# One block's keys and queries cast to fp16 before they are turned, in an attention and gated-FFN kernel

## The chip, the cores and the metric

The kernel runs on one core of one Trainium2 chip. The core has five instruction streams that run side by side and wait for each other by semaphores: PE (TensorE, matrix products), ACT (ScalarE), DVE (VectorE), POOL (GpSimd) and SP (SyncE, which here only issues loads and stores). The metric is the device time of one execution in microseconds (us), the median over several runs.

## What is computed

Inputs are q, k and v of 4 batches, 8 heads, 768 positions and 64 values per head, in fp32, and three weight matrices of a gated feed-forward layer. Cut to what matters:

```python
k_min, k_max = k_chunks.min(3), k_chunks.max(3)          # chunks of 32 positions
ub = sum(maximum(q * k_min, q * k_max))                  # bound of each query for each chunk
top_chunks = argsort(where(causal, ub, -1e9))[..., -6:]  # six chunks for each query
scores = where(sel & (i >= j), (q @ k.T) / 8, -1e9)
x = softmax(scores) @ v                                  # 3072 tokens of 512 values
out = (sigmoid(x @ w_gate) * (x @ w_val)) @ w_out        # d_ff 1536
```

The first 128 positions of a batch see at most four chunks, so nothing is chosen for them: they are plain causal attention.

## The kernel before

**Stages.** The 24 blocks of 128 tokens are spread over eight units of three blocks, u0 to u7. A unit is prepared (keys and queries turned so that the head's 64 values lie on partitions, bounds `ub`, the choice of chunks, masks), attended (scores `sc_`, `exp_`, causal mask `cm_`, products with the values `pv_`, division `rz_` and `x_`), and sent through the feed-forward layer (`g_`, `tanh_`, `v_`, `hg_`, and the output products `o0_`, `o1_`, `o2_`). While PE does the feed-forward products of one unit, the next is attended and a later one prepared. `attend(units[2], ...)`, for instance, is interleaved with `ffn(units[1], ...)`.

**The first blocks of the batches.** The first block of each batch, positions 0 to 127, goes through its own function `first` (L593): four of them, b = 0 to 3; the one of b = 3 belongs to unit u2. `load_first` (L519) loads its k and q in two halves each (`kf0_3`, `kf1_3`, `qf0_3`, `qf1_3`) and v (`vf_3`), as fp32. `kfT_3` and `qfT_3` (L603) turn k and q on PE, by four products each with a 128x128 identity, into a PSUM bank; `kf16_3` (ACT) and `qf16_3` (DVE) copy these to fp16 (L607); `scf_3` makes the scores, `expf_3_*` and `cmf_3_*` the masked weights (L655, L658), `pvf_3_*` the products with the values (L665). `vc_3` (POOL) casts the values to fp16 (L631).

**Order.** Nothing is scheduled at run time. Each operation is entered with a list of engines that could do it, a cost for each, a priority and the buffers that it reads and writes (`plan.add`, L49). A planner has turned this into the long string `ORDER` (L94 to L273): a list of names, each with the buffers' numbers behind a colon and with `@ENGINE` where it isn't the first engine of its list. The names are issued in this order (`Plan.order`, L78), so each engine runs its own names in order, and a name whose inputs aren't ready holds up all later names of its engine. A buffer kind has a few numbered places (`ps`: 8 PSUM banks; `np`: 7 places for fp16 copies; `v`: 6 for landed blocks), and whoever is given a place waits until its last holder's users are done.

**POOL's queue around the block.** POOL does the causal masks (`cm_`, L879: a mask of the diagonal blocks of each head's weights, without which `pv_` of that head can't finish), casts of the values (`v16_`, L567), copies of keys and queries into the operands of the score products (`hk`, `hq`, `hqm`, all through the helper `copy`, whose lines are L345 for ACT, L347 for DVE, L349 for POOL), and loads of weights. Before the change its names run here in this order:

```
... k16_1_1 v16_0_5 hq1_u3_0 vc_3 hk1_1_3 hk0_1_3 cm_u2_7 v16_1_0 hq0_u3_0 hk1_1_1 cm_u2_0
cm_u2_6 hqm0_u3_2 hk1_1_0 cm_u2_4 hk1_1_2 hk0_1_2 hkp111 cmf_3_0 cmf_3_1 ...
```

Here `hq*_u3_*` and `hk*_1_*` are queries and keys of unit 3 and batch 1, `cm_u2_h` the mask of head h of unit 2. In unit 2 (blocks 4 and 5 of batch 0) a `pv_u2_h` is eleven products, 5 for the first block and 6 for the second; the last one of each block reads the masked diagonal.

**Pattern copies.** `hkp1eo` (L166) copies a constant pattern of 64 partitions x 1536 fp16 values from the operand of even batches to that of odd batches, four copies in all: `hkp110` and `hkp101` on DVE, `hkp100` and `hkp111` on POOL. Unit 3 is the first that reads them.

**PE's queue around the block**: `... ub_u3 pv_u2_1 sc_u2_4_1 kfT_3 sc_u2_4_0 g_u1_10 v_u1_10 sc_u2_6_0 g_u1_11 v_u1_11 sc_u2_6_1 o0_u1_0 o1_u1_0 qfT_3 sc_u2_6_2 sc_u2_4_2 pv_u2_0 sc_u3_1_1 sc_u3_1_0 o2_u1_0 o0_u1_1 pv_u2_7 pv_u2_4 ...`

Of the kernel before, what the change touches and what calls it, by code (L numbers as in the profile page):

```python
# [112 lines left out]
hq1_u1_1@POOL kx1_u2_3:1 ap1_u1 sc_u1_1_0:0,2 qm_u2_0@POOL:0 tanh_u0_1 v_u0_1:5 hg_u0_0 qm_u2_2@ACT kx1_u2_2
g_u0_2:4,2,2 hq1_u1_0@POOL kt_u2_2@DVE:1 hq0_u1_2@POOL kx1_u2_0 v_u0_2:3 tanh_u0_2 apt1_u1 hq0_u1_3@POOL exp_u1_1_0
g_u0_3:6,3,3 kx0_u2_2 v16_0_1 hg_u0_1 sc_u1_0_1:4,3 wo0 v_u0_3:2 hg_u0_2 tanh_u0_3 hk0_u2_3@ACT hkp110 sc_u1_0_0:0
hk1_u1_0@POOL exp_u1_0_1 g_u0_4:5,0,4 exp_u1_0_0 kx0_u2_0 sc_u1_3_2:6,1 kt_u2_0@DVE:2 sc_u1_2_2:3,0 sc_u1_3_1:4
exp_u1_3_2 sc_u1_2_0:0 qm_u2_1 exp_u1_3_1 kT_u2_1:7 qm_u2_3 v_u0_4:6 exp_u1_2_0 kx1_u2_1 kx0_u2_1 sc_u1_3_0:4 cm_u1_2
g_u0_5:0,1,5 hg_u0_3 exp_u1_3_0 hkp100@POOL v_u0_5:2 kt_u2_1:0 hq1_u2_3 tanh_u0_5 g_u0_6:4,2,6 tanh_u0_4 hq0_u2_1@POOL
hg_u0_5 sc_u1_0_2:7 v_u0_6:0 kcr_u2@POOL exp_u1_0_2 hg_u0_4 cm_u1_3 hqm1_u1_2@ACT sc_u1_1_2:5 cm_u1_0 g_u0_7:2,3,7
v16_0_3 v_u0_7:7 tanh_u0_7 wo2 tanh_u0_6 g_u0_8:6,1,8 hg_u0_7 hq0_u2_3 cm_u1_1 ub_u2:2,4 hq1_u1_3@DVE tanh_u0_8  # L120
hq0_u2_0@POOL exp_u1_2_2 hk1_u2_0@POOL sc_u1_2_1:7 v_u0_8:6 hqm1_u1_0 exp_u1_2_1 k11_1 exp_u1_1_2 g_u0_9:3,0,9
hq1_u2_1@POOL hg_u0_8 v_u0_9:7 tanh_u0_9 sc_u1_1_1:5 g_u0_10:6,3,10 hg_u0_9 ubn1_u2:0 v_u0_10:3 v16_0_2 tanh_u0_10
exp_u1_1_1 g_u0_11:7,1,11 v11 hg_u0_10 pv_u1_3:4 ubn0_u2 tanh_u0_11 pv_u1_2 mx1_u2:0 pv_u1_0:6 hk0_u2_1@ACT
sc_u1_5_2:5,1 v_u0_11:3 hk0_u2_2 exp_u1_5_2 hg_u0_6 hk1_u2_2@ACT wm_23 hg_u0_11 pv_u1_1 sc_u1_6_1:1,3 sc_u1_5_0:2
hq0_u2_2@DVE exp_u1_6_1 sc_u1_7_1:7,0 rz_u1_1:0 sc_u1_5_1:5 x_u1_1:1 exp_u1_7_1 sc_u1_6_0:0 rz_u1_0:0 exp_u1_6_0
sc_u1_4_1:3,2 hkp101 exp_u1_5_0 sc_u1_4_0:1 o0_u0_0:4,0 kcr1 mx0_u2 k10_1 exp_u1_5_1 xps_u1_1:7,1 cm_u1_5 o1_u0_0
hq1_u2_2 ap1_u2 exp_u1_4_1 ap0_u2 sc_u1_7_0:0 x_u1_0:0 sc_u1_6_2:2 o2_u0_0 exp_u1_7_0 apt1_u2:0 exp_u1_6_2
hqm1_u2_0@DVE exp_u1_4_0 xps_u1_0:5 o0_u0_1:3,1 osb_u0_0@DVE cm_u1_4 apt0_u2 out_u0_0 o1_u0_1 cm_u1_6 hqm0_u2_2@ACT
cm_u1_7 sc_u1_4_2:6 pv_u1_5:0 hqm0_u2_0 q01_1:1 exp_u1_4_2 pv_u1_6:2 sc_u1_7_2:1 hqm1_u2_2 kf0_3:5 pv_u1_4 exp_u1_7_2
sc_u2_1_0:4,1 rz_u1_2:0 sc_u2_3_2:6,3 xT_u1_0 sc_u2_3_0:1 exp_u2_1_0 x_u1_2:2 pv_u1_7 o2_u0_1 exp_u2_3_0 cm_u2_1  # L130
rz_u1_3:0 x_u1_3:1 exp_u2_3_2 xT_u1_1 sc_u2_1_1:5 k16_1_2:5 sc_u2_2_0:4,2 kx1_1_3:0 exp_u2_1_1 sc_u2_7_1:0,0
xps_u1_3:1 q10_1 xps_u1_2:2 k16_1_3:3 exp_u2_2_0 sc_u2_3_1:6 k16_1_0@DVE:2 q00_1 o0_u0_2:7,0 osb_u0_1 cm_u2_3 kt_1_3:0
hk0_u2_0@ACT cm_u2_2 o1_u0_2 exp_u2_7_1 xT_u1_3 xT_u1_2@ACT kx0_1_0 o2_u0_2 v_0_4:2 kx1_1_0 g_u1_0:5,0,12 v_u1_0:4
kt_1_0:6 tanh_u1_0 g_u1_1:3,3,13 kx0_1_1 sc_u2_2_1:0 v_0_5:4 v_u1_1:1 exp_u2_2_1 hg_u1_0 q11_1 g_u1_2:2,2,14 tanh_u1_1
kx0_1_2 hk1_u2_1@ACT v_u1_2:5 vf_3:1 exp_u2_3_1 kx0_1_3 osb_u0_2 g_u1_3:0,1,15 tanh_u1_2 sc_u2_7_0:4 tanh_u1_3
v_u1_3:3 hg_u1_2 kx1_1_2 sc_u2_1_2:6 v16_0_4 g_u1_4:7,0,16 vf1_3:4 kx1_1_1 sc_u2_2_2:2 k16_1_1:1 qf1_3:3 v_u1_4:0
tanh_u1_4 exp_u2_2_2 g_u1_5:5,2,17 v16_0_5 out_u0_2 hg_u1_4 kf1_3 v_u1_5:7 hg_u1_3 tanh_u1_5 out_u0_1 kt_1_2:2
exp_u2_1_2 g_u1_6:2,0,0 k11_2:0 sc_u2_7_2:0 hg_u1_5 v_1_0:0 v_u1_6:3 tanh_u1_6 qf0_u3_2:0 g_u1_7:5,1,1 hg_u1_6
pv_u2_2:6 qf0_u3_1 tanh_u1_7 pv_u2_3 qf0_u4_0:1 exp_u2_7_2 sc_u2_0_0:7,3 hk0_1_0@DVE v_u1_7:2 exp_u2_7_0 qf0_u3_3
exp_u2_0_0 g_u1_8:3,2,2 kcr_1 qf0_u3_0 qm_u3_2@ACT:0 sc_u2_0_1:5 hg_u1_1 v_u1_8:0 qf0_3 hq1_u3_0@POOL tanh_u1_8  # L140
qf0_u4_3 g_u1_9:4,0,3 qm_u3_0 k10_2 vc_3 kt_1_1:5 k01_2 v_u1_9:7 tanh_u1_9 hk1_1_3 sc_u2_0_2:1 hg_u1_7 ub_u3:3,4
exp_u2_0_2 hg_u1_8 hk0_1_3 exp_u2_0_1 cm_u2_7 pv_u2_1:2 ubn0_u3:0 sc_u2_4_1:1,2 v16_1_0 kfT_3:0 k00_2 qf0_u4_2
hq0_u3_0@POOL ubm0_u3 sc_u2_4_0:5 ubn1_u3 g_u1_10:3,3,5 kf16_3:3 mx0_u3:0 hk1_1_1 hq0_u3_2@ACT v_u1_10:4 hg_u1_9
cm_u2_0 sc_u2_6_0:0,1 exp_u2_4_0 ap0_u3 g_u1_11:7,1,4 v_1_1:2 tanh_u1_10 apt0_u3:0 v_u1_11:5 tanh_u1_11 ubm1_u3
hg_u1_10 hk0_1_1@ACT sc_u2_6_1:3 mx1_u3 o0_u1_0:7,0 hqm0_u3_0@ACT hg_u1_11 o1_u1_0 rz_u2_1:0 ap1_u3 exp_u2_6_0
qf0_u4_1 x_u2_1:0 qfT_3:4 exp_u2_6_1 q00_2:1 cm_u2_6 apt1_u3 sc_u2_6_2:5 hq1_u3_2@ACT hqm0_u3_2 sc_u2_4_2:0 pv_u2_0
hk1_1_0 rz_u2_0:0 exp_u2_6_2 sc_u3_1_1:6,3 qf16_3@DVE:1 exp_u2_4_2 sc_u3_1_0:3 o2_u1_0 x_u2_0:1 cm_u2_4 exp_u2_4_1
kx0_2_2 o0_u1_1:5,1 hk1_1_2 osb_u1_0 exp_u3_1_0 hqm1_u3_0@DVE hk0_1_2 out_u1_0 pv_u2_7:4 kx1_2_3:0 pv_u2_4:0 v_1_3:4
xps_u2_1:2,0 sc_u2_5_1:1,0 v_1_2:1 xT_u2_1@ACT hkp111@POOL hqm1_u3_2@DVE exp_u3_1_1 scf_3:7,3,2 o1_u1_1 q10_2
exp_u2_5_1 q11_2 pv_u2_6 expf_3_0 sc_u2_5_2:2 o2_u1_1 expf_3_1:1 cmf_3_0 rz_u2_3:0 x_u2_3:2 exp_u2_5_2 kx0_2_0 cmf_3_1  # L150
sc_u2_5_0:6 k16_2_0@ACT:0 pvf_3_0:1 sc_u3_0_0:7,2 v16_1_1 xps_u2_0:3 sc_u3_0_2:4 kx1_2_2 exp_u2_5_0 o0_u1_2:2,0
exp_u3_0_2 cm_u2_5 osb_u1_1 rzf_3_0:0 o1_u1_2 xT_u2_0 q01_2 cm_u3_1 kx0_2_3 exp_u3_0_0 v16_1_3 sc_u3_0_1:6 kt_2_0:5
v16_1_2 exp_u3_0_1 cm_u3_0 xf_3_0:0 pvf_3_1:4 sc_u3_1_2:3 pv_u2_5 sc_u3_2_1:5,0 xps_u2_3:7 o2_u1_2 exp_u3_2_1
k16_2_1:2 rz_u2_2:0 exp_u3_1_2 rzf_3_1:1 out_u1_1 x_u2_2:1 xT_u2_3@ACT xpsf_3_0:6 xf_3_1:2 pv_u3_1:1 xTf_3_0@ACT
sc_u3_3_0:5,1 kx1_2_0 sc_u3_3_1:3 xps_u2_2:0 pv_u3_0 xT_u2_2@ACT xpsf_3_1:7 sc_u3_5_0:4,2 rz_u3_0:0 xTf_3_1
k16_2_3@DVE:6 exp_u3_5_0 sc_u3_3_2:6 v_1_4:0 x_u3_0:0 exp_u3_3_1 sc_u3_6_0:0,3 g_u2_0:7,2,7 v_u2_0:4 hk1_2_0@ACT
kx1_2_1 g_u2_1:3,0,8 exp_u3_3_2 kt_2_1:1 exp_u3_3_0 tanh_u2_1 v_u2_1:1 kx0_2_1 k16_2_2@ACT:3 hg_u2_1 g_u2_2:6,3,9
tanh_u2_0 v_u2_2:5 kcr_2@POOL k11_3:0 osb_u1_2 cm_u3_5 qf1_u4_2 g_u2_3:3,1,10 qf1_u4_1 k01_3 exp_u3_6_0 qf1_u4_0
qf1_u4_3 qf0_u5_3:0 qm_u4_0@ACT:0 qm_u4_2@POOL kt_2_2:0 tanh_u2_2 v_u2_3:7 sc_u3_6_2:1 k00_3 exp_u3_6_2 hg_u2_0
g_u2_4:2,0,6 hq0_u4_0@ACT hq0_u4_2@POOL qf0_u5_0 tanh_u2_3 v_u2_4:0 xps_u3_0:6,1 ub_u4:1,4 qf0_u5_1 cm_u3_6  # L160
xT_u3_0@ACT hk0_2_2@DVE tanh_u2_4 hk0_2_1 k10_3 qf0_u5_2 g_u2_5:3,2,11 hg_u2_4 hq1_u4_2@POOL ubn0_u4:0 v_u2_5:6
ubm0_u4 cm_u3_3 ubn1_u4 v_1_5:5 hk1_2_2 hg_u2_3 g_u2_6:2,0,12 hg_u2_2 v_u2_6:0 hq1_u4_0@POOL pv_u3_3:1 kt_2_3:4
# [1091 lines left out]
```

## Time and profile before

| what | value |
|---|---|
| median of 3 runs | 285.15 us (285.08 to 285.25) |
| the profiled execution | 285.57 us |
| its span | 283.7 us, granted TensorE clock 1.0 |
| PE busy | 270.4 us, 95% |
| DVE, ACT, POOL busy | 234.3, 208.1, 115.4 us |
| HBM read, written | 30.67 and 6.29 MB |

All positions in time below are microseconds from the start of the span. A row of an engine's order of time gives the start, the duration, engine, line, operation, output<-inputs, shapes and how many; in square brackets stands how long the engine was idle before it and what ended that. The chain of waits is followed back from the last instruction, and its pieces give a start, a duration and what ran. Starts in it can lie some 0.1 to 0.2 us behind those of PE's own order of time, because PE's instructions overlap.

### The profile page before, as it was taken

The page shows a single profiled execution, that of the slowest core. Times are in us where ns is not written, and L with a number is a line of the kernel's source. Part 1 is how long each engine was busy: PE and PEld are TensorE (multiplying, and loading weights), DVE is VectorE, ACT ScalarE, POOL GpSimd, SP SyncE. Part 2 cuts the span into 40 slices and gives each one's busy share as a digit, 9 for nine tenths or more (in the row PEclk, how much of TensorE's full clock was granted, in tenths as well). Part 3 has the DMA queues.
Part 4 walks back from the last instruction along what each step waited for, and adds up shares of the span by engine and source line. Part 5 has one row for each costly group of instructions (what it writes and reads, how often), then busy time and mean ns, then how long its engine had stood idle before and what let it go on. Part 6 is the DMA issues. An engine that isn't in the chain of part 4 may idle for free.

```text
span 283.7 us, 7050 instructions
## 1 busy us (share of the span) xinstructions
PE 270.4 (95%) x2602; PEld 171.0 (60%) x2602; DVE 234.3 (83%) x643; ACT 208.1 (73%) x438; POOL 115.4 (41%) x184
## 2 busy tenths in 40 slices
...
GB/s 173 254 252 201 196 200 216 167 206 178 229 171 183 199 154 159 217 168 227 166 54 2 31 116 94 64 14 2 0 0 31 104 91 12 76 0 0 2 73 149
DMA packets 130033, 34.26 MB, mean 121 GB/s; under 512 B 118096, under 2 KB 127056, under 8 KB 130000
## 3 DMA queue, kind: packets, MB, share of 16 engines
...
q8 instruction: 20, 0.33, 0.5%
q14 instruction: 13, 0.11, 0.1%
HBM read 30.67 MB, written 6.29 MB: 130 GB/s over the span
## 4 chain that ended last, share of the span: by engine, by line
PE 85%; DVE 4%; ACT 4%; issue 3%; POOL 2%; DMA 1%; DVEq 0%; POOLq 0%
PE o_u L981 22%; PE sc_u L862 11%; PE v_u L950 11%; PE g_u L950 11%; PE pv_u L895 6%; PE suv_u6u L1059 3%; PE sug_u6u L1059 3%; PE ube_u L801 3%; PE suv_u4u L1059 2%; PE sug_u4u L1059 2%; PE srg_u6u L1059 1%; PE srv_u6u L1059 1%; PE srv_u4u L1059 1%; PE srg_u4u L1059 1%; DMA kq_u<-in_q_dram 1%
## 5 line engine op out<-in xcount | busy, mean ns | idle before, releaser
L873 ACT ACTIVATE att_u<-sc_u 128x512 f16<-128x512 f32 (+3 forms) x184 | 90.4, 550 | 17.9 <-PE sc_u L862 17.0
L879 POOL TENSOR_SCALAR_AFFINE_SELECT att_u<-att_u 128x384 f16<-128x384 f16 (+1 forms) x56 | 28.5, 519 | 73.7 <-ACT att_u L873 52.4
L981 PE MATMUL o_u<-wo,hg_u 128*128 128x512 f16 x216 | 52.8, 379 | 0.0
L950 PE MATMUL v_u<-xT_u,wv 128*128 128x384 f16 x192 | 39.1, 326 | 0.1
L950 PE MATMUL g_u<-xT_u,wg 128*128 128x384 f16 x192 | 39.0, 326 | 0.0
L981 PEld LDWEIGHTS <-hg_u 128*128 128x128 f16 x216 | 20.0, 98 | 18.8 <-issue 0.6
L958 ACT ACTIVATE gate_u<-g_u 128x384 f16<-128x384 f32 x48 | 22.9, 494 | 11.0 <-PE g_u L950 9.3
L962 DVE SCALAR_TENSOR_TENSOR hg_u<-gate_u,v_u 128x384 f16<-128x384 f16 x48 | 25.1, 537 | 6.9 <-PE v_u L950 3.9
L862 PE MATMUL sc_u<-hqe,hke 128*128 128x128 f16 (+2 forms) x220 | 29.0, 243 | 0.0
L895 PEld LDWEIGHTS <-att_u 128*128 128x128 f16 x640 | 25.0, 98 | 4.9 <-issue 0.5
L862 PE MATMUL sc_u<-hqo,hko 128*128 128x128 f16 (+2 forms) x220 | 27.4, 243 | 0.0
L895 PE MATMUL pv_u<-v,att_u 128*128 128x65 f16 x640 | 27.2, 193 | 0.1
L950 PEld LDWEIGHTS <-wv 128*128 128x128 f16 x192 | 18.3, 98 | 10.9 <-issue 0.6
L950 PEld LDWEIGHTS <-wg 128*128 128x128 f16 x192 | 18.2, 98 | 10.6 <-issue 0.2
L862 PEld LDWEIGHTS <-hke 128*128 128x128 f16 x220 | 17.2, 98 | 7.3 <-issue 0.4
L862 PEld LDWEIGHTS <-hko 128*128 128x128 f16 x220 | 16.6, 98 | 6.5 <-issue 0.8
L567 POOL CAST v<-v 128x512 f16<-128x512 f32 x23 | 14.9, 662 | 12.4 <-DMA v<-in_v_dram 8.1
L990 ACT ACTIVATE osb_u<-o_u 128x512 f32<-128x512 f32 (+1 forms) x13 | 7.8, 597 | 13.9 <-PE o_u L981 13.9
L981 PE MATMUL o_u<-wo,hgp_u 128*128 128x512 f16 (+1 forms) x72 | 16.2, 370 | 0.0
L914 DVE TENSOR_TENSOR x_u<-pv_u,rz_u 128x384 f16<-128x384 f32 (+1 forms) x28 | 14.8, 531 | 0.4
L1059 PEld LDWEIGHTS <-Sv 128*128 128x128 f16 x96 | 9.0, 98 | 6.2 <-issue 0.3
L824 DVE MAX8 mx_u<-ubn_u 128x8 f32<-128x8 f32 (+16 forms) x152 | 12.6, 158 | 0.1
...
## 6 DMA issues: line engine op xcount, KB each, us to landing
...
kf<-in_k_dram SPq DMA_DIRECT2D x8, 128.0 KB, 3.9
```

Of the source, the lines that this page charges most:

```text
L567: plan.add(f"v16_{b}_{ib}", {POOL: pool(H * D)}, lambda e: nc.gpsimd.tensor_copy(v16[b % 2][:, ib, :, 0:D], at(t)), reads=[t], writes=[("v ...
L824: nc.vector.max(at(mx)[:, e_, j, :], at(ubn)[:, e_, j, 0:max(8, u.seen[j])])
L862: nc.tensor.matmul(at(t)[:, o:o + 128 * m], hk[b % 2][e_][:, p, 128 * jb:128 * jb + 128], hq[u.side][e_][:, p, 128 * x:128 * (x + m)], sta ...
L873: plan.add(f"exp_{u.name}_{h}_{y}", {ACT: act(n)}, lambda e, t=t, att=att, b0=b0, n=n: nc.scalar.activation(at(att)[:, b0:b0 + n], at(t), ...
L879: nc.gpsimd.affine_select(out=dv, in_=dv, compare_op=ALU.is_ge, fill=0.0, base=0, pattern=[[0, u.m], [1, 128]], channel_multiplier=-1)
L895: nc.tensor.matmul(at(pv)[:, last, x, :], at(att)[:, c:c + 128], v16[b % 2][:, jb, h, :], start=(jb == 0), stop=(jb == ib))
L914: plan.add(f"x_{u.name}_{p}", {DVE: dve(u.t)}, lambda e: nc.vector.tensor_tensor(at(x_).rearrange("p a (e d) -> p e a d", e=2), at(pv)[:, ...
L950: nc.tensor.matmul(at(t), w16[:, c, 128 * fb:128 * fb + 128], at(u.xt)[:, c, :], start=(c == 0), stop=(c == 3))
L958: plan.add(f"tanh_{u.name}_{fb}", {ACT: act(T)}, lambda e, g=g, gate=gate: nc.scalar.activation(at(gate), at(g), AF.Tanh, scale=0.5), read ...
L962: plan.add(f"hg_{u.name}_{fb}", {DVE: dve(T)}, lambda e, w_=w_, gate=gate, hg=hg: nc.vector.scalar_tensor_tensor(at(hg), at(gate), 1.0, at ...
L981: nc.tensor.matmul(at(o), hgs[c][1][1]()[:, 128 * tb:128 * tb + 128], wo16[:, fc, lo:hi], start=(c == 0), stop=(c == NFB - 1))
L1059: nc.tensor.matmul(at(t), left[i](c), right[i](c), start=first and c == 0, stop=c == 1, skip_group_check=not first)
```

## The change

For b = 3 alone, k and q are cast from fp32 to fp16 as they have landed, by two new operations `kc_3` and `qc_3` (each reads both halves, and may run on POOL, DVE or ACT; both are given to POOL), and the turns read these casts, with an fp16 identity and an fp16 PSUM bank. Values are rounded to fp16 before the turn and no longer behind it.

```diff
         for n in "kq":
-            t = ps(f"{n}fT_{b}", "pr", [128, NP, 128])
-
-            def turn(e, t=t, n=n):
+            src, keys, dt, ident = raw[n], [(raw[n], 0), (raw[n], 1), "ident32"], F32, ident32
+            if b == 3:
+                src = Buf("np", f"{n}c_{b}", [128, H, D], F16)
+                plan.add(f"{n}c_{b}", {POOL: pool(512), DVE: dve(512, 2), ACT: act(512, False)}, lambda e, src=src, n=n: copy(e, at(src), at(raw[n])),
+                         reads=keys[:2], writes=[src], prio=next_())
+                keys, dt, ident = [src, "ident16"], F16, ident16
+            t = ps(f"{n}fT_{b}", "pr", [128, NP, 128], dt)
+
+            def turn(e, t=t, src=src, ident=ident):
                 for p in range(NP):
-                    nc.tensor.transpose(at(t)[:, p], at(raw[n])[:, 2 * p:2 * p + 2].rearrange("s e d -> s (e d)"), ident32)
-
-            plan.add(f"{n}fT_{b}", pe(440, 230), turn, reads=[(raw[n], 0), (raw[n], 1), "ident32"], writes=[t], prio=next_())
+                    nc.tensor.transpose(at(t)[:, p], at(src)[:, 2 * p:2 * p + 2].rearrange("s e d -> s (e d)"), ident)
+
+            plan.add(f"{n}fT_{b}", pe(224 if b == 3 else 440, 230), turn, reads=keys, writes=[t], prio=next_())
             half[n] = Buf("np", f"{n}f16_{b}", [128, NP, 128], F16)
-            plan.add(f"{n}f16_{b}", {ACT: act(512), DVE: dve(512)}, lambda e, t=t, h=half[n]: copy(e, at(h), at(t)),
+            plan.add(f"{n}f16_{b}", {ACT: act(512), DVE: dve(512, 2 if b == 3 else 1)}, lambda e, t=t, h=half[n]: copy(e, at(h), at(t)),
```

`ORDER` is planned anew with this. Most of its text differs, but taken engine by engine, PE, ACT, SP and the weight loads keep their order name for name. Two queues differ. DVE loses `hkp110` (it stood between `hg_u0_2` and `kx0_u2_0`) and `hkp101` (between `rz_u1_0` and `kcr1`). POOL's differs so (the names between are the same):

```diff
-cm_u1_2 hkp100 hq0_u2_1
+cm_u1_2 hq0_u2_1
...
-v16_0_2 v11 cm_u1_5
+v16_0_2 v11 hkp100 cm_u1_5
...
-hqm0_u2_0 hqm1_u2_2 cm_u2_1 k16_1_2 k16_1_3 cm_u2_3 cm_u2_2 v16_0_4
+hqm0_u2_0 hqm1_u2_2 hkp110 cm_u2_1 k16_1_2 k16_1_3 cm_u2_3 cm_u2_2 hkp101 v16_0_4
...
-k16_1_1 v16_0_5 hq1_u3_0 vc_3 hk1_1_3
+k16_1_1 v16_0_5 kc_3 hkp111 hq1_u3_0 qc_3 vc_3 hk1_1_3
...
-hk1_1_2 hk0_1_2 hkp111 cmf_3_0
+hk1_1_2 hk0_1_2 cmf_3_0
```

The buffers' numbers change widely, since a swap of two banks is carried through to the end. Followed from holder to holder, 18 of 1049 buffers come behind another holder than before, among them `kfT_3` (now behind `sc_u2_0_1`), `sc_u2_4_1` and `sc_u2_4_0` (behind `v_u1_7` and `v_u1_8`), `qf16_3` (behind `kt_1_3`), `k16_2_0` (behind `qc_3`) and the loads `v_1_2`, `v_1_4`, `v_1_5` and `v_2_3`.

More of the change, by code (lines that the diff above doesn't have):

```diff
@@ L113 @@
[L113 to L162, printed above, removed]
```

285 lines of the change are left out of this document (167 added, 118 removed).

## The prediction

> **What bounds the kernel now.** I read the page first, then busy time by stretches, then the chain of waits, then each engine's order of time around the changed block. The profiled execution took 285.57 us, of which 283.7 are the span; the median of the runs is 285.15, so 0.42 less than the profiled one. I work in the span and carry the difference over to the median.
>
> ```profile
> PE 270.4 (95%) x2602; PEld 171.0 (60%) x2602; DVE 234.3 (83%) x643; ACT 208.1 (73%) x438; POOL 115.4 (41%) x184
> ...
> 120.00:160.00 40.00, 39.94 (x489) 26.80 (x488) 38.15 (x122) 35.99 (x73) 26.75 (x39) 1.00 0.59 117
> 160.00:200.00 40.00, 39.88 (x464) 26.62 (x461) 37.82 (x97) 36.01 (x76) 15.62 (x23) 1.00 0.20 52
> ```
>
> The columns of the last two rows are the stretch, its length, then PE, PEld, DVE, ACT, POOL busy, granted clock, DMA share and GB/s. TensorE (PE) is idle for 0.18 us in these 80, at full clock. So a microsecond that PE loses or gains near 85 us goes almost whole to the end, as long as nothing else holds it up there. PE and ACT keep their order of operations; only POOL and DVE have theirs changed.
>
> The chain of waits has the two turns that the change makes cheaper, an fp16 turn of another stage beside them, and the product of the unit's head 0 right behind the second (start, duration, what):
>
> ```profile
> 61.50 0.34 PE xps_u L927 x6
> ...
> 64.64 0.65 PE g_u L950 x4
> ...
> 81.74 0.44 PE kfT L603 x4
> 82.18 0.22 PE sc_u L862 x3
> ...
> 87.17 0.44 PE qfT L603 x4
> ...
> 87.93 0.33 PE pv_u L895 x11
> ...
> 100.26 0.65 PE g_u L950 x4
> ```
>
> **The change part by part.** *The turns.* Four fp32 identity products take 0.44 us, so 0.11 each; fp16 ones 0.34 / 6 = 0.057. Each of kfT_3 and qfT_3 falls to 0.22: PE gains 0.44 us, all of it on the path that sets the end, if nothing stalls. kf16_3 on ACT and qf16_3 on DVE (row at 88.40 below) read fp16 in place of fp32; at best they are shorter, and PE wants their result only at scf_3, three microseconds later, so I count nothing.
>
> *The two casts on POOL.* They are new, and they stand in a queue that runs in order. This is the step I take to decide. POOL now, and the loads on SP (the last two rows: us from issue to landing):
>
> ```profile
> 71.09 0.62 POOL L567 CAST v<-v 128x512 f16<-128x512 f32 x1
> 77.63 0.82 POOL L349 CAST hqo<-qf_u 64x768 f16<-64x768 f32 x1 [5.93 <-DVE qf_u L768]
> 78.52 0.76 POOL L349 CAST vf<-vf 128x512 f16<-128x512 f32 x1
> ...
> 81.46 0.61 POOL L567 CAST v<-v 128x512 f16<-128x512 f32 x1
> 82.01 0.82 POOL L349 CAST hqe<-qf_u 64x768 f16<-64x768 f32 x1
> ...
> 83.79 0.41 POOL L879 TENSOR_SCALAR_AFFINE_SELECT att_u<-att_u 128x256 f16<-128x256 f16 x1
> 87.22 0.41 POOL L879 TENSOR_SCALAR_AFFINE_SELECT att_u<-att_u 128x256 f16<-128x256 f16 x1 [3.03 <-ACT att_u L873]
> ...
> 89.25 0.41 POOL L879 TENSOR_SCALAR_AFFINE_SELECT att_u<-att_u 128x256 f16<-128x256 f16 x1
> ...
> 91.36 1.46 POOL L349 COPY hko<-hko 64x1536 f16<-64x1536 f16 x1
> ```
>
> ```profile
> 72.30 0.42 SPq L530 DMA_DIRECT2D kf<-in_k_dram  x1
> ...
> 77.24 0.58 SPq L530 DMA_DIRECT2D qf<-in_q_dram  x1
> ...
> kf<-in_k_dram SPq DMA_DIRECT2D x1, 128.0 KB, 3.2
> ...
> qf<-in_q_dram SPq DMA_DIRECT2D x1, 128.0 KB, 5.1
> ```
>
> The second half of the keys lands at 72.30 + 3.2 = 75.5. POOL is idle then, so kc_3 (0.6) and hkp111 (1.46) run from 75.5 to 77.6, and hq1_u3_0 starts at 77.6 as before. Next in the queue is qc_3, ahead of vc_3, and the second half of the queries lands only at 77.24 + 5.1 = 82.34. POOL stands still from 78.5 to 82.3. Behind it wait vc_3, hk1_1_3, hk0_1_3, cm_u2_7, v16_1_0, hq0_u3_0, hk1_1_1 and cm_u2_0, in this order; the first starts at 78.52 and the last ends at 83.79 + 0.41 = 84.20 now. The cast costs between 0.55 (from 81.46 to the next start at 82.01) and 0.76 (the row at 78.52); I take 0.60, nearest to the 0.61 and 0.62 of two of the three casts of this size. So vc_3 starts at 82.34 + 0.06 + 0.60 = 83.00 (0.06 is an estimate for the step from landing to start, from the 0.05 that POOL's mask needs to reach PE below), 4.48 late, and cm_u2_0 ends at 84.20 + 4.48 = 88.68.
>
> cm_u2_0 masks the diagonal blocks that pv_u2_0 reads, the 11 products at 87.93 in the chain, 87.77 in PE's order of time. How such a wait looks, from a later unit (POOL's mask ends at 192.71 + 0.52 = 193.23, six of the eleven products start 0.05 later; the first five read blocks that need no mask):
>
> ```profile
> 192.71 0.52 POOL L879 TENSOR_SCALAR_AFFINE_SELECT att_u<-att_u 128x384 f16<-128x384 f16 x1
> ...
> 193.28 0.36 PE pv_u L895 x6
> ```
>
> ```profile
> 87.77 0.50 PE L895 MATMUL pv_u<-v,att_u 128*128 128x65 f16 x11
> ...
> 90.22 0.83 PE L895 MATMUL pv_u<-v,att_u 128*128 128x65 f16 x22
> ```
>
> In pv_u2_0 the first masked block is the fifth product; four run before it at 0.33 / 11 = 0.03 each. It began at 87.77 + 0.12 = 87.89 and can begin at 88.68 + 0.05 = 88.73: PE is **0.84 us later** than before at this point. Since that is a fixed time, the 0.44 that the turns save has only lengthened the wait to 1.28 us, and up to 1.28 us of other delay on PE before it would cost nothing.
>
> POOL is still behind afterwards, but not so that PE feels it: cm_u2_4, at 89.25 now, follows cm_u2_0 without POOL's 3.03 of idle time, so it ends at 89.66 - 3.03 + 4.48 = 91.11, while its reader, in the second half of the 22 products at 90.22, stands at 90.55 + 0.84 = 91.39. The queue is 1.45 late there and gets 1.46 back because hkp111 has left 91.36. The masks of block 3 that follow wait for ACT.
>
> *The pattern copies.* hkp110 and hkp101 go from DVE to POOL, hkp100 and hkp111 elsewhere on POOL. DVE is spared 0.56 each (row at 53.13), in front of idle time that ends with PE (59.13): nothing.
>
> ```profile
> 53.13 0.56 DVE L347 COPY hke<-hke 64x1536 f16<-64x1536 f16 x1
> ...
> 59.13 0.20 DVE L912 RECIPROCAL rz_u<-pv_u 128x6 f32<-128x6 f32 x1 [1.69 <-PE pv_u L895]
> ...
> 63.33 0.31 DVE L347 COPY xT_u<-xps_u 128x384 f16<-128x384 f16 x1
> ...
> 88.40 0.66 DVE L347 CAST qf<-qfT 128x512 f16<-128x512 f32 x1
> ```
>
> ```profile
> 60.16 0.41 POOL L879 TENSOR_SCALAR_AFFINE_SELECT att_u<-att_u 128x256 f16<-128x256 f16 x1 [0.70 <-ACT att_u L873]
> 60.51 1.59 POOL L349 CAST k<-k 128x768 f16<-128x768 f32 x2
> ```
>
> On POOL, hkp110 stands ahead of the 60.16 row: 1.46 less 0.70 of idle time makes the key casts 0.8 late, and DVE's turn of the last of them and xT_u1_3 at 63.33 with it. That ends at 63.64 now, and the g product of unit 1 that reads it stands at 64.64: 1.0 of room for 0.8. hkp100 and hkp101 fall where POOL has nothing to do. If the room is gone (0.2 us lost at most), the later wait swallows it.
>
> *A shared resource.* Two DVE copies of one shape, the second beside hkp111, took 0.51 and 1.39:
>
> ```profile
> 90.20 0.51 DVE L347 COPY hqo<-apt_u 64x640 f16<-64x640 f16 x1
> ...
> 91.62 1.39 DVE L347 COPY hqo<-apt_u 64x640 f16<-64x640 f16 x1
> ...
> 76.07 0.31 DVE L347 COPY hke<-kt 64x768 f16<-64x768 f16 x1
> ...
> 79.62 0.97 DVE L962 SCALAR_TENSOR_TENSOR hg_u<-gate_u,v_u 128x384 f16<-128x384 f16 x2
> ...
> 83.52 0.37 DVE L829 TENSOR_TENSOR ap<-ubn_u,mx_u 128x160 f16<-128x160 f32 x1
> ...
> 86.17 0.29 DVE L829 TENSOR_TENSOR ap<-ubn_u,mx_u 128x160 f16<-128x160 f32 x1
> ```
>
> So hkp111 delays a copy by about 0.88, and the change moves it from 91.4 to 76.2, beside the copy at 76.07. DVE's qm_u3_0 behind that copy then comes 0.9 to 1.5 later (1.46 is the whole of hkp111), and ub_u3 on PE, which reads it, at most that much: within the 1.28 us or 0.2 past it. At 91.6 DVE gets its 0.88 back, where PE does not wait for it. Both at nothing, with 0.2 kept for the range.
> The Trainium skill, "SBUF — State Buffer", section "Who interferes with whom", calls this an exclusive lock between DVE and GpSimd, held for a whole instruction, also against DVE instructions with two SBUF inputs. The 1.39 row agrees. By that rule the two ap rows can hold up POOL's late queue too; by the sum above they cost nothing. The third rival prices it.
>
> *Buffers.* 417 of 1049 buffers carry another number, but only 18 follow another holder. The tightest, sc_u2_4_0, waits for a bank that DVE frees at 79.62 + 0.97 = 80.59, and PE wants it behind kfT_3, at 82.18; the loads v_1_2, v_1_4, v_1_5 and v_2_3 are issued after 90 and their new holders are done before. Nothing.
>
> **Sum**: 0.84 at pv_u2_0, less 0.1 that later short waits of PE may absorb (0.18 idle in the two stretches above): +0.75. Span 284.45, a profiled run of 286.3, median **285.9**.
>
> **The rivals.**
> *The queries land in time* (not slower): the wait vanishes if the landing is 1.28 us earlier, at 81.06, which is 3.8 after its issue. For: the keys took 3.2. Against: the queries were issued behind other loads and took 5.1, and SP's order is unchanged. Then PE keeps its 0.44: 285.15 - 0.44 = 284.7.
> *The wait is absorbed*: PE is late at 88.7, but DVE and ACT, 38 and 36 of 40 busy later, catch up meanwhile and PE runs without its small waits. For: those shares. Against: 0.18 us of idle PE. 285.2.
> *POOL's late queue is held up by DVE as well*: the ap rows at 83.52 and 86.17 fall into it, 0.37 + 0.29 = 0.66 more on cm_u2_0: 0.75 + 0.66 = 1.4, so 286.55. Against: masks and copies of POOL beside them kept 0.41 and 0.82 before.
> *The turns do not get cheaper*: with PE waiting for cm_u2_0 anyway this changes nothing unless the first rival holds, and then the time is 285.15.
>
> **How the numbers follow.** The forecast has 0.52 (its own range 285.4 to 286.4: landing 0.4 either way, cast 0.55 to 0.76), the early landing 0.20 (0.03 of it with turns that are no cheaper), the absorbed wait 0.12, the held-up queue 0.16. From the lowest rival to the third: 284.6 to 286.7. A measurement tells 0.2% (0.57 us) from no change. Slower by more: the third rival and four fifths of the forecast, 0.58. Within: a fifth of the forecast, the absorbed wait and about half of the early landing, since 0.44 is under 0.57: 0.30. Faster: the rest, 0.12.
>
> **What would show it.** POOL idle near 78.5 to 82.3 with the load of qf as its releaser; a wait of PE near 87.5, in the middle of pv_u2_0, released by POOL's mask and about 1.3 long; turns of 0.22 in the chain; the g product that now stands at 100.26 some 0.8 later. It is wrong if qc_3 starts before 81.1, if pv_u2_0 doesn't wait, or if PE's later rows don't stay late.

## The result, and the profile after

| kernel | runs | median, us | from, to |
|---|---|---|---|
| before | 21 | 285.07 | 284.62 to 286.23 |
| changed | 21 | 285.63 | 284.81 to 287.16 |

The changed kernel is slower by 0.25%: the ratio is 1.0025 [1.0015, 1.0034], which on 285.15 is 285.86 us, +0.71 (the two medians of the table alone differ by 0.56). The profiled execution of the changed kernel, though, took 285.02 us, one of the shortest of its 21, with a span of 283.1. It must be read with two further profiles of the same kernel, taken below as `e12_again` and `e1_again`.

A measure that serves through all that follows: the **stretch** from the first `g` product of unit 1 to the first of unit 2, in PE's own order of time. It holds the changed turns and the suspected wait, and little else of it differs; behind it, the rest of the span takes 183.6 us in nearly all profiles (183.55 to 183.65; 183.84 and 184.08 in two). The stretch itself starts somewhere between 63.68 and 65.43 us, with the moved pattern copies and without; this scatter lies ahead of the wait, goes into the time as well, and blurs the medians. Before the change the stretch was 35.61. The kernel before, then the changed kernel, PE's order of time (start, duration, engine, line, operation, shapes, count):

```profile
64.48 0.81 PE L950 MATMUL g_u<-xT_u,wg 128*128 128x384 f16 x4
...
100.09 0.81 PE L950 MATMUL g_u<-xT_u,wg 128*128 128x384 f16 x4
```

```profile
64.11 0.81 PE L955 MATMUL g_u<-xT_u,wg 128*128 128x384 f16 x4
...
99.55 0.81 PE L955 MATMUL g_u<-xT_u,wg 128*128 128x384 f16 x4
```

So 35.44 after the change: this execution gained 0.17 there. The chain of waits of the same kernel shows the pieces that stood in the prediction's first chain (start, duration, what):

```profile
81.38 0.22 PE kfT L608 x4
...
83.34 0.77 PE g_u L955 x4
...
86.70 0.22 PE qfT L608 x4
...
87.26 0.47 PE pv_u L900 x11
```

The turns take 0.22 instead of 0.44, as forecast. Two pieces are longer than before: a `g` product's group, 0.77 instead of 0.65, and `pv_u2_0`, 0.47 instead of 0.33. The second is all that is left in this execution of the forecast wait. POOL's order of time (in brackets: idle time before, and what ended it) and SP's say why:

```profile
76.47 0.61 POOL L348 CAST kc<-kf 128x512 f16<-128x512 f32 x1 [5.16 <-DMA kf<-in_k_dram]
77.03 1.49 POOL L348 COPY hko<-hko 64x1536 f16<-64x1536 f16 x1
78.58 0.97 POOL L348 CAST hqo<-qf_u 64x768 f16<-64x768 f32 x1
81.30 0.61 POOL L348 CAST qc<-qf 128x512 f16<-128x512 f32 x1 [1.74 <-DMA qf<-in_q_dram]
81.86 0.61 POOL L348 CAST vf<-vf 128x512 f16<-128x512 f32 x1
...
86.88 0.76 POOL L884 TENSOR_SCALAR_AFFINE_SELECT att_u<-att_u 128x256 f16<-128x256 f16 x2
```

```profile
77.32 1.15 SPq L529 DMA_DIRECT2D qf<-in_q_dram  x1
```

```profile
qf<-in_q_dram SPq DMA_DIRECT2D x1, 128.0 KB, 3.8
```

`qc_3` does wait for the second half of the queries with the whole queue behind it, but here they landed at 77.32 + 3.8 = 81.1 instead of 82.3, so POOL stood still for 1.74 us and not for 3.8. The first of the two masks at 86.88 is `cm_u2_0`. That is the first rival's landing, nearly to the tenth, and the reason why this one execution doesn't show what the median shows.

### The profile page after: what moved, and what is told of

Its sections match the earlier page's. It is cut to its first block, busy times and chain, and to the rows that moved or that the text cites. A ratio compares the mean times of both kernels' runs of the same rounds, so it can differ in the third digit from the quotient of the medians.

```text
span 283.1 us, 7049 instructions
## 1 busy us (share of the span) xinstructions
PE 269.7 (95%) x2602; PEld 170.3 (60%) x2602; DVE 232.7 (82%) x641; ACT 208.1 (73%) x438; POOL 119.3 (42%) x188
## 4 chain that ended last, share of the span: by engine, by line
PE 85%; DVE 4%; ACT 3%; issue 3%; DMA 1%; POOL 1%; SPq 0%; DVEq 0%; POOLq 0%
PE o_u L986 22%; PE sc_u L867 11%; PE v_u L955 11%; PE g_u L955 11%; PE pv_u L900 6%; PE suv_u6u L1064 3%; PE sug_u6u L1064 3%; PE ube_u L806 3%; PE suv_u4u L1064 2%; PE sug_u4u L1064 2%; PE srg_u6u L1064 1%; PE srv_u6u L1064 1%; DMA kf<-in_k_dram 1%; PE srv_u4u L1064 1%; PE srg_u4u L1064 1%
## 5 line engine op out<-in xcount | busy, mean ns | idle before, releaser
L955 PEld LDWEIGHTS <-wg 128*128 128x128 f16 x192 | 18.2, 98 | 10.7 <-issue 0.2
L996 DVE TENSOR_SCALAR osb_u<-o_u 128x512 f32<-128x512 f32 x11 | 7.5, 687 | 6.9 <-PE o_u L986 6.8
```

The source lines that it names most:

```text
L955: nc.tensor.matmul(at(t), w16[:, c, 128 * fb:128 * fb + 128], at(u.xt)[:, c, :], start=(c == 0), stop=(c == 3))
```

## The experiments

Two theories stood against each other. That of the prediction: the time is lost because `qc_3` holds POOL's queue until the queries land, and `cm_u2_0` behind it makes PE wait. The main rival: the time is lost by the four pattern copies that changed their places, through DVE, or through `hkp111` behind a cast that waits for the keys. The expectations call the first A and the second B; A2 in them is that `hkp111`, standing behind a cast that waits for the keys, runs late beside DVE's preparation of unit 3. Ratios are to the kernel before, run on the same chip in the same session. The stretches of all profiles, with the time at which the second half of the queries landed (issue + transfer):

| profile | stretch | landed | ratio, 95% |
|---|---|---|---|
| before | 35.61 | 82.3 | |
| changed | 35.44 | 81.1 | 1.0025 [1.0015, 1.0034] |
| `e1_again`: the changed kernel | 36.78 | 83.6 | 1.0011 [0.9983, 1.0039] |
| `e12_again`: the changed kernel | 37.89 | 83.3 | 1.0062 [1.0028, 1.0096] |
| `e4_qf_late` | 39.60 | 83.5 | 1.0168 [1.0126, 1.0211] |
| `e9_late_masks_first` | 38.42 | 85.0 | 1.0082 [1.0051, 1.0112] |
| `e6_qf_early` | 35.52 | 78.2 | 1.0033 [1.0006, 1.0061] |
| `e2_qc_late` | 36.10 | 83.3 | 1.0027 [1.0000, 1.0055] |
| `e3_hkp_only` | 35.62 | 80.4 | 1.0012 [0.9990, 1.0035] |
| `e5_casts_only` | 35.31 | 81.3 | 1.0015 [0.9991, 1.0040] |
| `e10_casts_only`: the same | 35.52 | 83.9 | 0.9976 [0.9949, 1.0002] |
| `e7_hkp111_first` | 35.30 | 81.9 | 1.0023 [0.9991, 1.0055] |
| `e11_hkp111_first`: the same | 35.30 | 81.7 | 0.9989 [0.9953, 1.0025] |
| `e8_best` | 36.69 | 78.8 | 1.0008 [0.9977, 1.0039] |

### The changed kernel again

No edit; it ran with each of two groups.

> The changed kernel unaltered, for a second profile. Theory A (POOL's queue: qc_3 waits for the second half of the queries, cm_u2_0 comes late behind it, PE waits in pv_u2_0): the time of an execution follows the landing of that load. In the first profile of the changed kernel it landed at 81.1 us, 3.8 after its issue, and that execution was among the shortest; in a profile with a later landing the start of the g product of unit 2 should be later one to one, beyond about 81.1 us. Median about 0.25% over the kernel before. Theory B (the four pattern copies on POOL): the same median, but no tie to the landing. Theory C (other bank holders): the same, and PE's lost time lies somewhere other than at pv_u2_0.

> The changed kernel a third time, for its time beside e10 and e11 on one chip and for a third landing. Theory A: the stretch is 35.3 us as long as the queries land before about 81, and longer by the delay beyond that (35.44 at 81.1, 36.78 at 83.6 with PE 0.9 later at the start of the stretch); the median 1.002 to 1.003 of the kernel before and 0.3% over e10 and e11.

The wait is there in both. In `e12_again` it ends the chain of waits, which can be read piece by piece from the transfer to the product:

```profile
79.32 3.97 DMA qf<-in_q_dram
...
83.50 0.61 POOL qc L348
84.11 0.56 POOL vf L348
...
84.76 0.80 POOL hko L348
...
85.62 0.87 POOL hke L348
86.49 0.36 POOL att_u L884
86.84 0.56 POOL v L566
87.41 0.78 POOL hqe L348
...
88.23 0.83 POOL hko L348
...
89.13 0.41 POOL att_u L884
...
89.59 0.39 PE pv_u L900 x7
```

These are, in their order, `qc_3`, `vc_3`, `hk1_1_3`, `hk0_1_3`, `cm_u2_7`, `v16_1_0`, `hq0_u3_0`, `hk1_1_1` and `cm_u2_0`: the queue that the prediction lists. PE's order of time of the same execution, and of `e1_again`:

```profile
86.91 0.29 PE L900 MATMUL pv_u<-v,att_u 128*128 128x65 f16 x4
89.59 0.39 PE L900 MATMUL pv_u<-v,att_u 128*128 128x65 f16 x7 [2.40 <-POOL att_u L884]
```

```profile
88.35 0.28 PE L900 MATMUL pv_u<-v,att_u 128*128 128x65 f16 x4
89.94 0.39 PE L900 MATMUL pv_u<-v,att_u 128*128 128x65 f16 x7 [1.30 <-POOL att_u L884]
```

Four products run and the fifth waits, 2.40 and 1.30 us. The busy time by stretches tells the same (length, PE, PEld, DVE, ACT, POOL busy, granted clock, DMA share, GB/s); first the profile of the section above, then `e12_again`:

```profile
84.00:100.00 16.00, 16.00 (x189) 10.58 (x188) 14.36 (x44) 14.24 (x30) 12.10 (x21) 1.00 1.07 186
```

```profile
84.00:100.00 16.00, 13.60 (x148) 8.44 (x147) 11.81 (x36) 12.76 (x26) 13.84 (x24) 1.00 1.07 187
```

PE lacks 2.40 of 16 us, and nothing else in it stands still. The ratio of `e12_again`, 1.0062, is more than twice what I had expected; that of `e1_again`, 1.0011, is under it, and its interval includes no change.

### Queries landing later and earlier

The load is moved by one place on SP's queue, later in `e4_qf_late`, earlier in `e6_qf_early`:

```diff
 # e4_qf_late, SP
-k11_2 v_1_0 qf0_3 k10_2 k01_2
+k11_2 v_1_0 k10_2 qf0_3 k01_2
 # e6_qf_early, SP
-k11_2 v_1_0 qf0_3 k10_2 k01_2
+qf0_3 k11_2 v_1_0 k10_2 k01_2
```

> The changed kernel with the load of the second half of the queries one place later on SP, behind one load of keys (384 KB); qc_3 keeps its place in POOL's queue. Those loads took 1.5 to 2 us of SP each in the two profiles. Theory A: the landing is that much later, PE's wait in pv_u2_0 grows by as much, and the time is 1.5 to 2 us over the changed kernel. Theories B and C: as the changed kernel within 0.1%.

> The changed kernel with the load of the second half of the queries three places earlier on SP, ahead of the load of keys of batch 2 and of a block of values; qc_3 keeps its place in POOL's queue, and so do the pattern copies. Theory A: the landing is near 77 and POOL doesn't wait for it, so PE doesn't wait in pv_u2_0: the stretch from g of unit 1 to g of unit 2 is about 35.2 us, as for e5, and the time 0.9985. Theory A2: between 35.2 and 36.0, as hkp111 still follows kc_3. Theory B or C: as the changed kernel.

`e4_qf_late` is slower by 1.68% [1.26%, 2.11%]. Its POOL and PE in their order of time:

```profile
83.70 0.61 POOL L348 CAST qc<-qf 128x512 f16<-128x512 f32 x1 [4.42 <-DMA qf<-in_q_dram]
```

```profile
89.74 0.39 PE L900 MATMUL pv_u<-v,att_u 128*128 128x65 f16 x7 [2.43 <-POOL att_u L884]
...
90.36 3.57 PE L986 MATMUL o_u<-wo,hg_u 128*128 128x512 f16 x8
```

In this execution the queries landed 19.5 us behind the first `g` product of unit 1, in `e12_again` 19.4: the wait is that of `e12_again`, yet the stretch is 1.7 longer. The eight output products behind the wait took 3.57 us; in the profile of the changed kernel the same eight took 1.89. The stretches say why (the third number from the end is the granted clock):

```profile
91.00:92.00 1.00, 1.00 (x3) 0.29 (x2) 1.00 (x2) 0.00 (x0) 0.93 (x2) 0.50 0.00 0
```

The clock that PE was granted fell to half behind the wait. If the wait brought that about, it cost twice; the wait of `e12_again` didn't (last section). I had expected 1.5 to 2 us over the changed kernel; beside `e1_again` of the same session it is 1.57%, 4.5 us, of which the clock, by this profile, explains 1.7.

In `e6_qf_early` the queries landed at 78.2, and POOL never stood still for them:

```profile
80.31 0.61 POOL L348 CAST qc<-qf 128x512 f16<-128x512 f32 x1 [0.32 <-POOL hqo L348]
```

PE has no wait in `pv_u2_0` and the stretch is 35.52, so the wait goes when the landing does. The time doesn't follow: 1.0033 [1.0006, 1.0061]. In its profile 0.22 of the stretch are a `pv` that waits for a cast of the values, and the rest of the span is 0.24 longer than in most. That the moved load pushes the loads behind it back would fit, but no run shows it, and what costs the median is not settled.

### Masks ahead of the cast

`e4_qf_late` with two masks taken from behind `qc_3` to a place ahead of it:

```diff
-hq1_u3_0 qc_3 vc_3 hk1_1_3 hk0_1_3 cm_u2_7 v16_1_0 hq0_u3_0 hk1_1_1 cm_u2_0 cm_u2_6
+hq1_u3_0 cm_u2_7 cm_u2_0 qc_3 vc_3 hk1_1_3 hk0_1_3 v16_1_0 hq0_u3_0 hk1_1_1 cm_u2_6
```

> e4 (the load one place later) with the two masks cm_u2_7 and cm_u2_0 ahead of qc_3 in POOL's queue; all else of the queue still waits for the landing. Theory A: it is the mask behind the cast that PE waits for, so with the load as late as in e4 the 2.4 us in pv_u2_0 are gone; what is left is at most a shorter wait at the next score products, for hq0_u3_0, which in e4 ended at 88.3 where PE wants it near 87.4: some 0.6 us. PE's clock, which fell to 0.5 after the long wait of e4, stays at 1.0. The stretch from g of unit 1 to g of unit 2 falls from 39.6 to about 36 us and the time from 1.017 to 1.003 or less. Theories B and C: as e4.

POOL's order of time, then PE's (the bracket at `qc_3` names a semaphore of DVE, whose `hg_u` it doesn't read; the queries that it does read landed at 79.91 + 5.1 = 85.0):

```profile
79.71 0.77 POOL L884 TENSOR_SCALAR_AFFINE_SELECT att_u<-att_u 128x256 f16<-128x256 f16 x2
85.14 0.61 POOL L348 CAST qc<-qf 128x512 f16<-128x512 f32 x1 [4.66 <-DVE hg_u L967]
...
88.78 0.82 POOL L348 CAST hqe<-qf_u 64x768 f16<-64x768 f32 x1
```

```profile
87.13 0.50 PE L900 MATMUL pv_u<-v,att_u 128*128 128x65 f16 x11
89.65 0.55 PE L867 MATMUL sc_u<-hqe,hke 128*128 128x384 f16 x5 [2.03 <-POOL hqe L348]
...
93.14 0.38 PE L900 MATMUL pv_u<-v,att_u 128*128 128x65 f16 x7 [0.76 <-POOL att_u L884]
```

`pv_u2_0` runs its eleven products without a stop. The wait went to the next thing on PE that reads from the late queue, `sc_u3_1_1`, which needs `hq0_u3_0`: 2.03 us, and 0.76 later in `pv_u2_4` for `cm_u2_4`. So PE waits for whatever stands in POOL's queue behind `qc_3`. The stretch, 38.42, and the time, 1.0082, came down less than I had reckoned (about 36, and 1.003 or less). In this execution the landing was 1.5 us later than in that of `e4_qf_late`.

### The cast out of the way of the queue

`e2_qc_late` puts `qc_3` behind `cm_u2_0`; the pattern copies stay where the change put them.

```diff
-hq1_u3_0 qc_3 vc_3 hk1_1_3 hk0_1_3 cm_u2_7 v16_1_0 hq0_u3_0 hk1_1_1 cm_u2_0 cm_u2_6
+hq1_u3_0 vc_3 hk1_1_3 hk0_1_3 cm_u2_7 v16_1_0 hq0_u3_0 hk1_1_1 cm_u2_0 qc_3 cm_u2_6
```

> Only qc_3 is moved in POOL's queue, from ahead of vc_3 to behind cm_u2_0. Theory A: the wait of PE is gone and the gain of the turns stays: 0.44 us under the kernel before, so 0.9985 of it, about 1.1 us under the changed kernel's median, and a narrower spread. Theories B and C: as the changed kernel, 1.0025.

A miss on time: I expected faster, and it came out at 1.0027 [1.0000, 1.0055], beside 1.0011 for the changed kernel in the same session. In the profile the wait for `cm_u2_0` is gone, with the queries landing at 83.3. But PE loses 0.30 us up to `sc_u2_4_1`, most of it for a bank that DVE's `hg_u1_7` frees, and some 0.5 in the `g` and `v` products behind `kfT_3`, for banks that DVE frees late too. (The expectation of `e5_casts_only` below puts the first at `ub_u3`, for `qm_u3_0`; in PE's order of time the products of `ub_u3` follow each other as in the other profiles.) PE's, POOL's and DVE's order of time:

```profile
80.96 0.51 PE L900 MATMUL pv_u<-v,att_u 128*128 128x65 f16 x11
81.54 0.38 PE L867 MATMUL sc_u<-hqo,hko 128*128 128x256 f16 x2
```

```profile
77.77 0.61 POOL L348 CAST kc<-kf 128x512 f16<-128x512 f32 x1 [4.40 <-DMA kf<-in_k_dram]
78.32 1.49 POOL L348 COPY hko<-hko 64x1536 f16<-64x1536 f16 x1
```

```profile
75.38 0.58 DVE L773 STREAM_TRANSPOSE qf_u<-q 128x384 f32<-128x384 f32 x1 [0.95 <-DMA q<-in_q_dram]
...
77.86 0.62 DVE L581 TENSOR_TENSOR kcr<-kx,kcr 128x96 f32<-128x96 f32 x1
```

DVE stood still for 0.95 us for a load of another block's queries, and a small product of two tiles, `kcr_1`, took 0.62; in `e10_casts_only`, with no POOL instruction beside it, it took 0.21:

```profile
77.22 0.21 DVE L581 TENSOR_TENSOR kcr<-kx,kcr 128x96 f32<-128x96 f32 x1
```

What held `kcr_1` is the key cast `kc_3`, not `hkp111`: with 0.21 it would have been over at 78.07, and `hkp111` starts at 78.32. `kc_3` ends at 78.38 and `kcr_1` 0.10 later; in all seven profiles in which `kc_3` began at least 0.07 us before `kcr_1`, the end of `kcr_1` comes 0.10 to 0.15 behind that of `kc_3`. `hkp111` does the same to `qm_u3_0`: it took 0.46 here, where `hkp111` was nearly through, but 1.03 in `e6_qf_early` and 1.02 in `e1_again`, where it ended 0.34 behind `hkp111` (78.44 + 1.46 = 79.90):

```profile
79.22 1.02 DVE L590 TENSOR_SCALAR qm_u<-qf_u 128x640 f32<-128x640 f32 x1
```

In `e1_again` PE didn't feel that: the wait for `cm_u2_0` alone gives its stretch to 0.01 us (table below). In `e2_qc_late` the late load (0.95) and the cast (0.41) made DVE late together; no run parts the two, and how often that load is late is open.

### The pattern copies by themselves

`e3_hkp_only` is the kernel before, with its fp32 turns and no cast, and the four pattern copies on POOL in the places that the change gave them:

```diff
-cm_u1_2 hkp100 hq0_u2_1
+cm_u1_2 hq0_u2_1
...
-v11 cm_u1_5
+v11 hkp100 cm_u1_5
...
-hqm1_u2_2 cm_u2_1 k16_1_2 k16_1_3 cm_u2_3 cm_u2_2 v16_0_4
+hqm1_u2_2 hkp110 cm_u2_1 k16_1_2 k16_1_3 cm_u2_3 cm_u2_2 hkp101 v16_0_4
...
-v16_0_5 hq1_u3_0 vc_3
+v16_0_5 hkp111 hq1_u3_0 vc_3
...
-hk0_1_2 hkp111 cmf_3_0
+hk0_1_2 cmf_3_0
```

> The kernel before with only the four pattern copies placed as in the changed kernel (all on POOL), without the casts and with fp32 turns. Theory A: within 0.1% of the kernel before. Theory B: the whole loss and the 0.44 us of the turns on top, 1.004. Theory C: 1.000, since no buffer gets another holder here.

The stretch is 35.62 against 35.61. The time, 1.0012 [0.9990, 1.0035], is no different from 1 within its interval; 1.004, which the rival needs with fp32 turns, lies outside, but a loss of a few tenths of a us would be hidden. And without `kc_3` ahead of it `hkp111` ran at 71.4 here, not at 77.0 beside DVE's copies, so this run doesn't test the second form of the rival. That one is answered by the profiles of the changed kernel, where the wait for `cm_u2_0` leaves nothing of the stretch for it (table below).

### Casts without the moved copies, and the copy ahead of the cast

`e5_casts_only` and `e10_casts_only` are one kernel: both casts, `qc_3` behind `cm_u2_0`, and the pattern copies as before the change. `e7_hkp111_first` and `e11_hkp111_first` are one as well: `e2_qc_late` with `hkp111` ahead of `kc_3`.

```diff
 # e5, e10, against e2_qc_late: hkp110, hkp101 on DVE, hkp100 behind cm_u1_2, and
-v16_0_5 kc_3 hkp111 hq1_u3_0 vc_3 ... hk0_1_2 cmf_3_0
+v16_0_5 kc_3 hq1_u3_0 vc_3 ... hk0_1_2 hkp111 cmf_3_0
 # e7, e11, against e2_qc_late
-v16_0_5 kc_3 hkp111 hq1_u3_0 vc_3
+v16_0_5 hkp111 kc_3 hq1_u3_0 vc_3
```

> The changed kernel with the four pattern copies back where the kernel before has them (two on DVE, hkp111 late on POOL) and qc_3 behind cm_u2_0. In e2, PE got 0.3 us late at ub_u3, waiting for DVE's qm_u3_0, and 0.56 more in the g and v products behind kfT_3, while hkp111 ran on POOL from 78.3 to 79.8 beside DVE's copies. Theory A2 (the queue's wait, and beside it hkp111 that follows kc_3 and keeps DVE from a shared port): both losses are gone; the stretch from the first g product of unit 1 to that of unit 2 is 35.61 - 0.44 = 35.2 us, and the time 0.9985 of the kernel before. Theory A alone: 35.2 too, as for e2, where it was 36.1. Theory C (other bank holders): the loss behind kfT_3 stays, 35.6 to 36.1.

> e2 with hkp111 ahead of kc_3 on POOL instead of behind it, so that it runs from about 72 to 73.5, where POOL has nothing else, and no longer beside DVE's copies near 76 to 80. Theory A2: DVE's qm_u3_0 is in time, the stretch is 35.2 to 35.4 us and the time 0.9985 to 0.999. Theory C: as e2, 36.1 and 1.0027.

> e5 again, for its time: in its profile the stretch was 35.31 us against 35.61 before, so 0.3 us were won; its runs spread too widely to show that. Theory A2: 0.999 of the kernel before, its stretch again near 35.3.

> e7 again, for its time: 35.30 us in the stretch there. Theory A2: 0.999 of the kernel before, its stretch again near 35.3.

In three of the four profiles the stretch is 35.30 or 35.31, the shortest of all and 0.31 below the kernel before; in the 35.52 of `e10_casts_only` 0.22 are again the `pv` that waits for a cast of the values. In `e10_casts_only` the queries landed at 83.9, later than in any profile of the changed kernel, and nobody waits for them; POOL's order of time:

```profile
85.33 0.41 POOL L884 TENSOR_SCALAR_AFFINE_SELECT att_u<-att_u 128x256 f16<-128x256 f16 x1
85.69 0.61 POOL L348 CAST qc<-qf 128x512 f16<-128x512 f32 x1
```

The mask comes first, and `qc_3` follows without idle time. The times say less. In one session the two were 1.0015 [0.9991, 1.0040] and 1.0023 [0.9991, 1.0055], in the next 0.9976 [0.9949, 1.0002] and 0.9989 [0.9953, 1.0025], there beside the changed kernel's 1.0062 [1.0028, 1.0096]. In that session neither interval overlaps the changed kernel's. The session before had no run of the changed kernel, and `e2_qc_late` showed no gain beside `e1_again`; so in the times the gain from moving the cast shows in one of the two sessions that have both. A gain over the kernel before isn't shown beyond the intervals. Nor do `e7_hkp111_first` and `e11_hkp111_first` show that `hkp111` was what made `e2_qc_late` slow: in their profiles DVE didn't wait for that load, and `kcr_1` took 0.21 and 0.27.

### Both loads early

`e8_best` is `e5_casts_only` with the second halves of the keys and the queries loaded ahead of the block's values:

```diff
 # SP
-vf_3 qf1_3 out_u0_2 kf1_3 out_u0_1 k11_2 v_1_0 qf0_3 k10_2
+qf1_3 kf1_3 qf0_3 vf_3 out_u0_2 out_u0_1 k11_2 v_1_0 k10_2
```

> e5 with both second halves, of keys and of queries, loaded three to seven places earlier on SP, ahead of vf_3. If what decides is the landings alone, it beats both kernels: 35.2 us in the stretch whatever the landings, 0.9985 of the kernel before, with the narrowest spread. If the loads that it pushes back (vf_3, the keys of batch 2) are wanted soon, it is slower than e5.

1.0008 [0.9977, 1.0039], and no gain. Its profile, with a stretch of 36.69, is of an execution in which POOL waited 7.2 us for one load of values (6.6 in `e5_casts_only`), and SP's loads were some 4 us later than there. They were so ahead of the moved loads already (two loads of values issued at 67.92 instead of 63.74), so the move didn't make those late; what it costs itself isn't settled.

## Why the prediction was right

**Time and direction.** 285.9 was forecast and 285.86 is measured, and the mechanism is the one forecast: `qc_3` waits on POOL, eight operations queue behind it, and the fifth product of `pv_u2_0` waits for the last of them. `e12_again` shows each link; in their profiles `e6_qf_early`, `e2_qc_late` and `e5_casts_only` take the wait away, and `e9_late_masks_first` moves it to another reader. In the times, `e4_qf_late` is slower than the changed kernel beside it, and `e10_casts_only` and `e11_hkp111_first` are faster; those of `e2_qc_late` and `e6_qf_early` show no gain. That forecast and measurement agree to 0.04 us is luck: the changed kernel stood at 1.0025, 1.0011 and 1.0062, that is 0.7, 0.3 and 1.8 us over the kernel before.

**The wait closes to two hundredths.** The fifth product would come 23.10 us behind the first `g` product of unit 1 if it waited for nothing (87.09 + 4 x 0.03 - 64.11 in the changed kernel's profile). What it is later than that is the delay, and 35.30, the stretch of the profiles in which nobody waits there, plus the delay should be the stretch (in the first row the start of the seven is an estimate, from the mask's usual 0.41 and the 0.05 from mask to product):

| profile | without a wait | seven products start | delay | 35.30 + delay | stretch |
|---|---|---|---|---|---|
| changed | 87.21 | 87.34 (86.88 + 0.41 + 0.05) | 0.13 | 35.43 | 35.44 |
| `e1_again` | 65.37 + 23.10 = 88.47 | 89.94 | 1.47 | 36.77 | 36.78 |
| `e12_again` | 63.92 + 23.10 = 87.02 | 89.59 | 2.57 | 37.87 | 37.89 |
| `e4_qf_late` | 64.04 + 23.10 = 87.14 | 89.74 | 2.60 | 37.90, + 1.68 of slow clock | 39.60 |

The delay is 0.17 more than the idle time in brackets, since the profile counts the four products ahead as busy until their modelled ends, 0.29 us for 0.12 of issue.

**From the landing to the mask** the sum was 82.34 to 88.68, 6.34 us. Measured from `qc_3`'s start to the mask's end: 81.30 to 87.29, 83.81 to 89.89, 83.50 to 89.54, 6.0 to 6.1 us instead of 6.28, more than half of it because `vc_3` took 0.61 and not 0.76; the step from landing to start took about 0.2 and not 0.06. Together 6.2 to 6.3 us: the two errors nearly cancel.

**The landing as a fixed number: the weakest step.** I took 82.34 from one profile. The three profiles of the changed kernel have 81.1, 83.6 and 83.3, with stretches 0.17 below, 1.17 above and 2.28 above that of before. Counted from unit 1's first `g` product, the landings come 17.0, 18.2 and 19.4 us later, and before the change it was 82.34 - 64.48 = 17.86. Carried over one to one from each of the three, a landing at 17.86 gives +0.7, +0.8 and +0.7 (-0.17 + 0.85, 1.17 - 0.33, 2.28 - 1.54), and the forecast was +0.75. So the sum was right for its landing, and the landing was one that happened to lie in the middle. The kernel before reads the same loads (5.1 us in its profile, 3.5 in `e3_hkp_only`), but wants the queries only at `qfT_3` (87.17). The early landing that I gave 0.20 as a rival is one of the three profiles: not a case against the others, but one end of a spread that every execution draws from.

**The term that was mis-sized** is "PE gains 0.44 us ... if nothing stalls". Where no wait covers it the gain is 35.61 - 35.30 = 0.31. Both turns are 0.22 shorter, but the `g` group at 83.34 takes 0.77 instead of 0.65. The changed kernel's DVE, order of time:

```profile
82.71 0.54 DVE L967 SCALAR_TENSOR_TENSOR hg_u<-gate_u,v_u 128x384 f16<-128x384 f16 x1
```

This is `hg_u1_9`, which ends at 83.25 and frees the bank of `v_u1_9` that `g_u1_11` writes. PE now comes there 0.22 earlier than before, and DVE doesn't. That this bank is what ended the 0.12 is read from the buffers' numbers and the row; no run of its own shows it. For the time it mattered little: with `cm_u2_0` late, PE's gain only lengthens the wait, as the prediction said.

**The pattern copies** were put at nothing, and `e3_hkp_only` agrees within its interval. The details were partly off. DVE's order of time in the changed kernel:

```profile
62.87 0.98 DVE L757 STREAM_TRANSPOSE kt<-k 128x768 f16<-128x768 f16 x1 [0.71 <-POOL k L348]
63.78 0.32 DVE L346 COPY xT_u<-xps_u 128x384 f16<-128x384 f16 x1
...
76.54 0.65 DVE L581 TENSOR_TENSOR kcr<-kx,kcr 128x96 f32<-128x96 f32 x1
...
90.74 0.87 DVE L346 COPY hqo<-apt_u 64x640 f16<-64x640 f16 x1
```

`hkp110` makes DVE wait 0.71 us for the key casts, 0.8 having been reckoned; `xT_u1_3` ends at 64.10, and the fourth product of the group at 64.11, the one that reads it, starts near 64.6 (64.11 + 3 x 0.16), so some 0.5 of the room is left. `hkp111` (77.03 to 78.52) didn't touch the copy of keys, which I had named (now at 75.81), because the keys landed too late for the two to meet. What DVE met was `kc_3`, a meeting that the prediction doesn't reckon with: `kcr_1` took 0.65 instead of 0.21. The copy at 90.74, which had taken 1.39 beside `hkp111`, takes 0.87, and 0.32 where POOL does nothing beside it (`e2_qc_late` at 92.20, `e3_hkp_only` at 90.82), so the 0.51 that I had compared with was held up too. The Trainium skill, "SBUF — State Buffer", section "Who interferes with whom", calls the ports that DVE and GpSimd share an exclusive lock, over which a DVE instruction with two SBUF inputs contends with a GpSimd instruction that reads SBUF. The trace agrees: `kcr_1` is such a one, it started 0.07 behind `kc_3` (76.47 + 0.61 = 77.08), and it ended 0.11 behind the end of `kc_3`.

**The rivals.** "Held up by DVE as well" falls by its size: behind the wait the queue ran faster than reckoned. In `e1_again` `hq0_u3_0` took 0.92 instead of 0.82 beside an `ap` row, so what there is of it is near 0.1 and not 0.66. "Absorbed" falls: what PE loses in the stretch isn't won back, as 183.6 us follow with the wait (`e12_again`) and without. "Turns no cheaper" falls with the chain's 0.22. Buffers cost nothing in the changed kernel's profiles but the bank above.
